# One list schedule over the whole kernel, changes of TensorE's tiling in its model, and a bank of its own for the last product

## The chip, the cores and the metric

The kernel runs on one core of one Trainium2 chip. The metric is the device time of one execution in microseconds (us); before the change it is 645.9 us, the median of three runs between 644.11 and 646.52. The profile of one further execution has a span of 646.7 us from the first to the last instruction. Times inside the kernel below are from that profile, counted from the start of its span.

## The reference, cut to what matters

Two blocks follow each other, all in 32-bit floats. The first is a linear recurrence over time for 4 batches and 8 heads of width 48, 768 steps long:

```python
for t in range(S):                      # state: (B, H, 48, 48)
    cur = einsum('bhd,bhe->bhde', u * k[t], v[t])
    y[t] = einsum('bhd,bhde->bhe', r[t], state + cur)
    state = w * state + einsum('bhd,bhe->bhde', k[t], v[t])
```

The second takes the result as 3072 tokens of 384 features, normalises each token and applies a gated layer of width 1536:

```python
xn = x / sqrt(mean(x * x) + 1e-6) * rms_g
out = (silu(xn @ w_gate) * (xn @ w_val)) @ w_out
```

## The kernel before: the parts that the change touches

Time is cut into 12 chunks of 64 steps, so a chunk is 256 tokens. For each chunk, a chain of small operations called *mixing* does the recurrence; its three large pieces on TensorE are named A (scores inside the chunk), Y (outputs) and U (the new state), and S stands here for the small products of the normalisation. Then the tokens go through the first layer in blocks here called R, and through the second in blocks called F. Chunks 0 and 1 are done one by one. Chunks 2 to 11 are done in five pairs, each with a form of Strassen's algorithm: seven products f1 to f7 for each of six groups of features, and seven products P1 to P7 for the second layer, in place of eight each.

The pieces of TensorE's work have four shapes, which the profile shows as rows times columns: A is 48\*64, Y is 128\*64 and 128\*48, U is 128\*48, R is 64\*128, and F and S are 128\*128. An R block is one product of the first layer:

```python
def product(ps_, w, x, start):
    for cc in range(CC):                 # 3
        for z in range(2):               # two halves of the rows
            rows = slice(64 * z, 64 * z + 64)
            pe.matmul(ps_[:, z, 0:NT], w[rows, cc, :], x[rows, cc, :], ...)
```

The order of all instructions is fixed when the program is built. Every operation is put into a list with its engine, an estimate of its cost, what it reads and writes; a list scheduler then simulates the engines, and picks on each engine the ready operation with the earliest deadline. Deadlines come backwards from *goals* for the products of the two layers:

```python
late = [goals.get(i, 1e6 + i) for i in range(n)]
for i in reversed(range(n)):
    for j in then[i]:
        late[i] = min(late[i], late[j] - self.hop(i, j) - self.ops[i][1])
```

There are two such lists, one after the other. The first (chunks 0 to 3 of mixing, chunks 0 and 1 of the layers, and the rounding of the weights) is improved by a random search over the goals; the second (all the pairs) is scheduled once:

```python
p.give(p.search(cells, 25.0, {"PE": 1.5, ...}, 3000), warm)

p = Plan()
... # all pairs; mixing and loads of the next pair go between the layers
p.give(p.schedule(p.goals_of(line, 0.0, 1.19), free, 0.5))
```

TensorE writes its products into six PSUM banks, two each named a, b and c, and two more for mixing. One group of a pair uses them like this (with VectorE's and ScalarE's readers left out except one):

```python
mm(xs_a, a_keys, a, wa[i][:, o], xa[s], True, "f1")
mm(["t2"], ["b"], b, late["s2"][i][:, o], t_of(2), True, "f2")
add("DVE", 0.69, ["b", "m1"], ["g1"], lambda: dve.tensor_add(gv[:, :, 1], b[sl], m1), name="g1")
mm(["t1"], ["c"], c, late["s1"][i][:, o], t_of(1), True, "f3")
mm(xn_a + [f"s3.{i}"], ["b"], b, wa[i + 2][:, o], xa[s + 1], False, "f4")
mm(xs_b, a_keys, a, wb[i][:, o], xb[s], False, "f5")
mm(["t4"], ["b"], b, wb[i + 2][:, o], t_of(4), False, "f6")
mm(xn_b, ["c"], c, late["s4"][i][:, o], xb[s + 1], False, "f7")
```

Here `t1`, `t2`, `t4` and the new `xa[s + 1]` are sums of the tokens of the pair, which VectorE makes after mixing. In the second layer of a pair:

```python
bank = {"x": bank_of["a"][:, 0], "w": bank_of["a"][:, 1], "y": bank_of["b"][:, 0], "z": bank_of["c"][:, 0]}
mm("x", h_keys[0], h[0], part(0, 0), True, "P1")
mm("z", gs + out_keys("o1"), sum_1, w2(0), True, "P5")
mm("x", h_keys[2], h[2], part(2, 0), False, "P2")
mm("y", ts + out_keys("o2"), sum_2, w2(1), True, "P6")
plus(["o1"], ["b", "m1"], results[:, 1], flat["y"], m1, "u2")
mm("y", h_keys[1] + out_keys("o3"), h[1], part(0, 1), False, "P7")
plus(["o3"], ["b", "m1"], results[:, 3], flat["y"], m1, "u3")
mm("w", h_keys[3] + out_keys("o4"), h[3], w2(2), True, "P4")
plus(["o2"], ["a1", "o3"], results[:, 2], flat["w"], results[:, 3], "c21")
plus(["o3"], ["c"], results[:, 3], flat["z"], results[:, 3], "c22")
mm("z", h_keys[2], h[2], part(2, 1), False, "P3")          # adds to P5 in the same bank
plus(["o1"], ["c"], results[:, 1], flat["z"], results[:, 1], "c12")
result(1, s, 1)                                            # the store to memory
```

P3 adds to the bank that holds P5, so it may start only when VectorE's `c22` has read P5 from there; `c22` comes after `u3`, which needs P7.

Of the kernel before, what the change touches and what calls it, by code (L numbers as in the profile page):

```python
# [50 lines left out]
P = 128  # L51
# [12 lines left out]
L = 64  # L64
# [30 lines left out]
class Plan:  # L95
# [3 lines left out]
    HOP = 0.2  # L99

    def __init__(self):
        self.ops, self.last, self.readers = [], {}, {}

    def add(self, engine, cost, reads, writes, give, land=0.0, port=False, name=""):
# [7 lines left out]
        self.ops.append((engine, cost, deps, give, land, port, name))  # L112
# [11 lines left out]
    def schedule(self, goals, free, patience=0.3):  # L124


        n = len(self.ops)
        then = [[] for _ in range(n)]
        for i, op in enumerate(self.ops):
            for d in op[2]:  # L130
                then[d].append(i)
        late = [goals.get(i, 1e6 + i) for i in range(n)]
        for i in reversed(range(n)):
            for j in then[i]:
                late[i] = min(late[i], late[j] - self.hop(i, j) - self.ops[i][1])
        free, port = dict(free), {"DVE": 0.0, "POOL": 0.0}
        missing = [len(op[2]) for op in self.ops]
# [4 lines left out]
        for _ in range(n):  # L142
            when, e = min((max(free[e], min(at[i] for i in ready[e])), e) for e in free if ready[e])
            i = min((i for i in ready[e] if at[i] <= when), key=lambda i: late[i])
            sooner = [j for j in ready[e] if at[j] <= when + patience and late[j] < late[i] - 1]
            if sooner:
                i = min(sooner, key=lambda j: late[j])
            s = max(when, at[i])
            if self.ops[i][5]:
                s = max(s, port["POOL" if e == "DVE" else "DVE"])  # L150
# [5 lines left out]
            for j in then[i]:  # L156
                at[j] = max(at[j], end[i] + self.hop(i, j))
                missing[j] -= 1
                if not missing[j]:
                    ready[self.ops[j][0]].add(j)  # L160
        return start

    def replay(self, start, free):

        free, port, end = dict(free), {"DVE": 0.0, "POOL": 0.0}, [0.0] * len(self.ops)
        for i in sorted(range(len(self.ops)), key=lambda i: (start[i], i)):
            e, cost, deps, _, _, locks, _ = self.ops[i]
            s = max([free[e]] + [end[d] + self.hop(d, i) + (1.0 if self.ops[d][0] == "SP" else 0.05) for d in deps])
            if locks:
                s = max(s, port["POOL" if e == "DVE" else "DVE"])  # L170
            free[e] = end[i] = s + cost * (1.0 if e == "PE" else 1.05)
            if locks:
                port[e] = end[i]
        return end
# [9 lines left out]
    def search(self, cells, first, free, trials):  # L184

        goals, rng, best = self.goals_of(cells, first, 1.0), random.Random(3), None
        for trial in range(trials):
# [5 lines left out]
            elif trial:  # L193
                new[rng.randrange(len(self.ops))] = rng.uniform(0, max(goals.values()))
            start = self.schedule(new, free)
            end = self.replay(start, free)
            end = max(end[i] for i in cells) + 0.3 * sum(end[i] for i in cells) / len(cells)
            if best is None or end <= best[0]:
                best, goals = (end, start), new
        return best[1]  # L200
# [13 lines left out]
def fast(ctx, tc, chan, tok, vpad, wka, wkb, wot, cols, u_row, out, bad):  # L214
# [417 lines left out]
    bank_keys = {"a": ["a0", "a1"], "b": ["b"], "c": ["c"]}  # L632
# [56 lines left out]
    def mixing(s):  # L689
# [3 lines left out]
        if quick:  # L693
            add("ACT", 1.6, ["w", "CHk0", "CHk1"], ["ku"], lambda: u_k(s, ku), name=f"ku {s}")
            for half in range(2):
                add(
                    "PE", 1.05, ["ku", "CHr0", "CHr1"], [f"a{half}"],
                    lambda half=half: products(bank_of["a"][:, half], half, ku, CH[:, 0], CH[:, 0]), name=f"E {s}",
                )
# [23 lines left out]
        if quick:  # L723
            for half in range(2):
                add("PE", 1.05, score_keys[half], [two[half][1]], lambda half=half: scores(half), name=f"A {s}")
        else:
            add(
                "PE", 2.35, score_keys[0] + score_keys[1], [two[0][1], two[1][1]], lambda: [scores(0), scores(1)],
                name=f"A {s}",
# [25 lines left out]
        else:  # L755
            add(
                "PE", 3.25, ["VSv"] + output_keys[0] + output_keys[1], [pair[0][1], pair[1][1]],
# [45 lines left out]
        for z in range(2):  # L803
# [3 lines left out]
            "PE", 1.9, ["KH0", "KH1", "VSv", "VSs0", "VSs1"] + [f"khd{z}{i}" for z in range(2) for i in range(HP)],  # L807
# [13 lines left out]
        "DVE", 0.86, ["pw"], ["o0"], lambda: [  # L821
# [4 lines left out]
    add("PE", 0.9, ["o0"], [key], lambda bank=bank: token_powers(bank), name="wk")  # L826
# [27 lines left out]
    def gate_val(s, i, o):  # L854
# [6 lines left out]
            lambda: product(ps_, wa[i][:, o], xa[s], True), name=f"g {s} {i} {o}",  # L861
# [3 lines left out]
            lambda: product(ps_, wb[i][:, o], xb[s], False), name=f"g {s} {i} {o}",  # L865
        ))
        add("ACT", 0.38, keys, [f"h{n}"], lambda: act.activation(h, ps_[:, 0, 0:NT], AF.Silu), name=f"silu {s}")
        add("DVE", 0.42, keys, [f"h{n}"], lambda: dve.tensor_mul(h, ps_[:, 1, 0:NT], h), name=f"hm {s}")
        return h, f"h{n}"

    def add_cell(s, i, hs):

        po, keys = next_bank()
        sums = rows_out[:, s]
# [9 lines left out]
        if i == 0:  # L884
            add("ACT", 0.8, keys, [f"o{s}"], lambda: act.copy(sums, po[:, :, 0:DM]), name=f"o {s}")
        else:
            add("DVE", 0.96, keys, [f"o{s}"], lambda: dve.tensor_add(sums, po[:, :, 0:DM], sums), name=f"o {s}")
# [693 lines left out]
```

## Time and profile before

| what | value |
|---|---|
| time, median of 3 | 645.9 us |
| span of the profile | 646.7 us |
| TensorE busy (of it matmuls of ones that only keep it busy in the first 25 us: 84 records) | 625.2 us |
| VectorE, ScalarE, GpSimd busy | 436.5, 349.0, 42.1 us |
| granted TensorE clock, mean | 0.991 |
| memory read and written | 58.69 MB and 4.72 MB |

Every operation is recorded through one helper, so all rows carry its line, L92; rows are told apart by the tiles they write and read and by their shapes. `bank_a`, `bank_b` and `bank_c` are written by the layers, `at` by mixing. TensorE is busy nearly all the time, so three things decide: the gaps in which it does nothing, the clock that it is granted, and whether its busy time is all needed. An idle time of another engine matters only where TensorE waits at its end.

### The profile page before, as it was taken

What the parts mean: (1) busy time and instruction counts of PE and PEld (TensorE: products, weight loads), DVE (VectorE), ACT (ScalarE), POOL (GpSimd) and SP (SyncE); (2) the same over time, 40 slices, a digit from 0 to 9 for tenths busy, and PEclk for the clock granted to TensorE, in tenths of its full rate; (3) what the DMA queues carried; (4) which work ended last, traced back from release to release, by engine and by line L of the source; (5) the groups of instructions that cost most, each with busy time, mean ns of one, the idle gap of its engine ahead of it and who ended that gap; (6) DMA issues with size and microseconds to landing.
All of it is one profiled execution on the core that took longest, in us unless ns stands there. A gap on an engine that the chain in (4) does not pass through costs nothing.

```text
span 646.7 us, 16003 instructions
## 1 busy us (share of the span) xinstructions
PE 625.2 (97%) x6882; PEld 549.6 (85%) x6882; DVE 436.5 (67%) x613; ACT 349.0 (54%) x914; POOL 42.1 (7%) x39
## 2 busy tenths in 40 slices
PE   9989999999999999999999999999999999899994
PEld 8868687877888998888898888898888899788894
DVE  7898877747785968774866666766676754555531
ACT  5796575634622878722887832696931694321200
POOL 3154440100000000000000000000000000000000
PEclk9989999999999999999999999999999999999997
DMA  8886641413200354600353501154501142100001
GB/s 261 303 303 220 185 153 51 117 47 88 107 11 2 111 168 121 190 22 1 82 201 98 166 1 66 51 170 148 153 27 50 43 118 63 35 1 1 2 15 41
DMA packets 21233, 64.54 MB, mean 100 GB/s; under 512 B 2720, under 2 KB 8480, under 8 KB 19744
## 3 DMA queue, kind: packets, MB, share of 16 engines
q1 hardware_dynamic: 21152, 63.42, 31.5%
q8 instruction: 56, 0.92, 0.6%
q14 instruction: 25, 0.20, 0.1%
HBM read 58.69 MB, written 4.72 MB: 98 GB/s over the span
## 4 chain that ended last, share of the span: by engine, by line
PE 88%; DVE 5%; DMA 3%; ACT 2%; issue 1%; SPq 0%; DVEq 0%; ACTq 0%
PE bank_b L92 29%; PE bank_a L92 25%; PE bank_c L92 23%; PE at L92 11%; DMA chan<-in_chan_dram 1%; DMA TOK<-in_tok_dram 1%; DVE rows_out L92 1%; DVE gv L92 1%; DVE ME L92 1%; ACT MO L92 1%; ACT ME L92 1%; DVE t L92 1%; DMA sq<-in_wot_dram 0%; DVE TOK L92 0%; DVE MO L92 0%
## 5 line engine op out<-in xcount | busy, mean ns | idle before, releaser
L92 DVE TENSOR_TENSOR gv<-bank_b,m 128x512 f32<-128x512 f32 x90 | 62.2, 691 | 47.8 <-PE bank_b L92 44.9
L92 PE MATMUL bank_b<-xa,wa 64*128 64x256 f32 x444 | 55.1, 381 | 3.6 <-DVE gv L92 2.4
L92 DVE TENSOR_TENSOR gv<-bank_c,gv 128x512 f32<-128x512 f32 x60 | 41.4, 690 | 16.2 <-PE bank_c L92 15.3
L92 PEld LDWEIGHTS bank_b<-xa,wa 64*128 64x128 f32 x444 | 42.0, 187 | 10.4 <-DVE gv L92 3.6
L92 ACT ACTIVATE gv<-gv 128x512 f32<-128x512 f32 (+1 forms) x60 | 30.7, 523 | 37.2 <-DVE gv L92 37.1
L92 ACT COPY m<-bank_a 128x512 f32<-128x512 f32 (+1 forms) x35 | 19.9, 570 | 56.9 <-DVE gv L92 42.9
L92 PE MATMUL bank_a<-xa,wa 64*128 64x256 f32 x396 | 49.1, 380 | 1.4 <-DVE rows_out L92 1.4
L92 PE MATMUL bank_a<-wo,h 128*128 128x192 f32 (+1 forms) x264 | 49.8, 345 | 0.5 <-ACT m L92 0.5
L92 ACT ACTIVATE sq<-sq 128x384 f32<-128x384 f32 x72 | 40.5, 562 | 16.9 <-DMA sq<-in_wot_dram 10.9
L92 PE MATMUL bank_a<-xb,wb 64*128 64x256 f32 x396 | 48.9, 379 | 0.0
L92 PEld LDWEIGHTS bank_a<-wo,h 128*128 128x128 f32 x264 | 43.2, 190 | 5.4 <-issue 1.3
L92 ACT ACTIVATE ME<-dmask,du 64x64 f32<-64x64 f32 x176 | 46.0, 331 | 2.8 <-DVE du L92 2.0
L92 ACT ACTIVATE MO<-dmask,du 64x64 f32<-64x64 f32 x176 | 46.7, 336 | 0.8 <-DVE du L92 0.2
L92 PE MATMUL bank_b<-t,s 64*128 64x256 f32 x360 | 44.1, 377 | 1.6 <-DVE t L92 1.6
L92 PE MATMUL bank_b<-t,wb 64*128 64x256 f32 x360 | 44.4, 379 | 0.0
L92 PE MATMUL bank_c<-xb,s 64*128 64x256 f32 x360 | 44.3, 378 | 0.0
L92 PEld LDWEIGHTS bank_a<-xa,wa 64*128 64x128 f32 x396 | 37.2, 187 | 8.1 <-DVE rows_out L92 3.0
L92 PE MATMUL bank_c<-t,s 64*128 64x256 f32 x360 | 44.1, 377 | 0.0
L92 ACT ACTIVATE gv<-bank_a 128x256 f32<-128x256 f32 x30 | 11.5, 384 | 58.2 <-PE bank_a L92 58.1
L92 PEld LDWEIGHTS bank_a<-xb,wb 64*128 64x128 f32 x396 | 37.8, 187 | 5.9 <-issue 1.8
L92 PEld LDWEIGHTS bank_b<-t,s 64*128 64x128 f32 x360 | 34.7, 187 | 6.0 <-DVE t L92 2.0
L92 PEld LDWEIGHTS bank_c<-xb,s 64*128 64x128 f32 x360 | 34.5, 187 | 5.1 <-issue 1.3
(143 smaller groups left out, 1289.3 us busy)
## 6 DMA issues: line engine op xcount, KB each, us to landing
chan<-in_chan_dram SPq DMA_DIRECT2D x11, 1024.0 KB, 6.8
TOK<-in_tok_dram SPq DMA_DIRECT2D x12, 768.0 KB, 4.8
VS<-in_vpad_dram SPq DMA_DIRECT2D x24, 336.0 KB, 4.9
raw<-in_wot_dram SPq DMA_DIRECT2D x8, 576.0 KB, 5.7
out_dram<-rows_out SPq DMA_DIRECT2D x48, 96.0 KB, 2.4
sq<-in_wka_dram SPq DMA_DIRECT2D x12, 384.0 KB, 3.0
sq<-in_wkb_dram SPq DMA_DIRECT2D x12, 384.0 KB, 3.2
sq<-in_wot_dram SPq DMA_DIRECT2D x12, 384.0 KB, 3.2
```

Of the source, the lines that this page charges most:

```text
L92: return lambda *args, **kwargs: self.tc.keep_in_program_order(give(*args, **kwargs))
```

## The change

1. **One schedule.** Both lists become one. The random search now looks at all operations up to the first product of the second pair, and is scored by the ends of all TensorE's operations; then everything is scheduled once. To make this possible many operations look up their tiles only when they are given out (`lambda: wa[i][:, o]`), and the keys of the tiles have the same names in both parts.
2. **Changes of tiling in the model.** Each TensorE operation is marked as using half the rows at a time (`rows=True`: R and A) or all of them (Y, U, F, S). A change of the mark costs 0.15 us in the model, and an operation that needs a change has to be more urgent by 2 us to be taken. The estimates for A, Y and U are lowered to 2.0, 2.85 and 1.58 us.
3. **Twice the time for the pairs' chains.** For operations of the pairs, deadlines are counted back with twice the cost and twice the hop between engines, so that long chains of small operations become urgent sooner.
4. **A bank for the last product.** P3 writes the second bank of c and no longer adds to P5 there; VectorE adds P5 in one operation more (`u4`). In the last pair P3 is given in two halves, each with its own addition and store, so that the first half's store can run beside the second half.

The purpose is that TensorE finds less time without work where one part meets the next, and changes its tiling less often.

The core of the diff (cuts are marked with `...`; left out are the renamed keys, the lambdas of point 1, and the moved lines around them):

```diff
     HOP = 0.2
+    SWITCH = 0.15
+    AHEAD = 30.0
+    KEEP = 2.0
...
-        for i in reversed(range(n)):
-            for j in then[i]:
-                late[i] = min(late[i], late[j] - self.hop(i, j) - self.ops[i][1])
+        early = min(goals[i] for i in goals if i >= relaxed) - self.AHEAD
+        for i in reversed(range(len(self.ops))):
+            by, cost = 2 if i >= relaxed else 1, self.ops[i][1]
+            for j, hop in self.then[i]:
+                due = late[j] - by * (hop + cost)
+                if i < relaxed <= j and due < early:
+                    due = early
+                if due < late[i]:
+                    late[i] = due
...
-            i = min((i for i in ready[e] if at[i] <= when), key=lambda i: late[i])
+            turn = (lambda i: late[i] + self.KEEP * (self.ops[i][7] != mode)) if e == "PE" else late.__getitem__
+            i = min((i for i in ready[e] if at[i] <= when), key=turn)
...
             s = max(when, at[i])
+            if e == "PE":
+                s += self.SWITCH * (self.ops[i][7] != mode)
+                mode = self.ops[i][7]
...
-        goals, rng, best = self.goals_of(cells, first, 1.0), random.Random(3), None
+        rng, best, last = random.Random(2), None, [i for i in range(count) if self.ops[i][0] == "PE"]
...
-                "PE", 2.35, score_keys[0] + score_keys[1], ..., name=f"A {s}",
+                "PE", 2.0, score_keys[0] + score_keys[1], ..., name=f"A {s}", rows=True,
...
-                "PE", 3.25, ["VSv"] + output_keys[0] + output_keys[1], ...     # Y
+                "PE", 2.85, ["VSv"] + output_keys[0] + output_keys[1], ...
...
-            "PE", 1.9, ["KH0", "KH1", "VSv", "VSs0", "VSs1"] + ...             # U
+            "PE", 1.58, ["KH0", "KH1", "VSv", "VSs0", "VSs1"] + ...
...
-    p.give(p.search(cells, 25.0, {"PE": 1.5, ...}, 3000), warm)
-    p = Plan()
...
-        keys = {"x": "a0", "w": "a1", "y": "b", "z": "c"}
+        keys = {"x": "a0", "w": "a1", "y": "b0", "z": "c0", "v": "c1"}
...
+        plus(["r1"], ["c0"], results[:, 1], flat["z"], results[:, 1], "u4")
...
-        mm("z", h_keys[2], h[2], part(2, 1), False, "P3")
-        plus(["o1"], ["c"], results[:, 1], flat["z"], results[:, 1], "c12")
-        result(1, s, 1)
+        for js in ((0, 1),) if s + 2 < NS else ((0,), (1,)):
+            mm("v", h_keys[2], lambda: h[2], part(2, 1), js[0] == 0, "P3", js)
+            to, x = (t[:, js[0] : js[-1] + 1] for t in (results[:, 1], flat["v"]))
+            plus(["r1"], ["c1"], to, x, to, "c12")
+            result(1, s, 1, js)
...
-    free = {"PE": 0.0, "DVE": 0.0, "ACT": 0.0, "POOL": 0.0, "SP": 0.0}
-    p.give(p.schedule(p.goals_of(line, 0.0, 1.19), free, 0.5))
+    goals = p.goals_of(cells, 25.0, 1.0) | p.goals_of(line, 150.0, 1.0)
+    n_searched = next(i for i in line if p.ops[i][6] == f"f1 {FIRST + 2} 0")
+    goals = p.search(cells, goals, free, n_searched, n_first, 3000)
+    p.give(p.schedule(goals, free, len(p.ops), n_first), warm)
```

## The prediction

> **What bounds the kernel now.** I read the busy times first, then TensorE's idle time and granted clock by stage, then the chain that ended last in order of time, and at the end the compiled order of TensorE's instructions in both kernels. The busy line:
>
> ```profile
> PE 625.2 (97%) x6882; PEld 549.6 (85%) x6882; DVE 436.5 (67%) x613; ACT 349.0 (54%) x914; POOL 42.1 (7%) x39
> ```
>
> TensorE is the bound; VectorE has a third of the span to spare. The work itself is not changed (258 R blocks, as many F blocks and as many A, Y and U in both compiled orders), so the change can only take from three things: the 21 us in which TensorE is idle, time under a lowered clock, and time lost inside the 625 us. The table by stage gives the first two (columns: length of the stage, busy time of each engine, granted clock, DMA share, GB/s):
>
> ```profile
> core 0: us, PE busy (x) PEld busy (x) DVE busy (x) ACT busy (x) POOL busy (x), PEclk, DMA share, GB/s
> 25.00:45.00 20.00, 16.37 (x287) 13.89 (x282) 18.08 (x25) 19.47 (x58) 7.71 (x7) 0.99 0.84 280
> 45.00:50.40 5.40, 5.40 (x14) 2.68 (x13) 5.30 (x9) 2.48 (x6) 3.06 (x3) 0.72 0.78 265
> 50.40:206.00 155.60, 155.60 (x1653) 127.06 (x1652) 115.98 (x160) 81.17 (x211) 24.14 (x16) 1.00 0.32 99
> 206.00:540.00 334.00, 330.21 (x3864) 298.58 (x3862) 229.05 (x303) 210.93 (x567) 0.00 (x0) 1.00 0.32 98
> 540.00:604.00 64.00, 61.38 (x534) 53.94 (x530) 34.71 (x56) 18.53 (x37) 0.00 (x0) 1.00 0.07 17
> 604.00:634.10 30.10, 27.16 (x172) 25.64 (x170) 12.87 (x15) 1.90 (x4) 0.00 (x0) 1.00 0.04 9
> 634.10:640.00 5.90, 5.85 (x24) 5.55 (x24) 0.00 (x0) 0.00 (x0) 0.00 (x0) 0.71 0.30 69
> ```
>
> Length minus PE busy is the idle time: 3.6 us in the opening, none from 45 to 206, 3.8 + 2.6 = 6.4 in the pairs, 2.9 in the last layer. From 634 the clock is 0.71. The chain shows what that means (columns: start, us, what):
>
> ```profile
> 624.45 3.90 PE bank_a L92 x24
> 628.35 3.91 PE bank_b L92 x24
> ...
> 632.28 0.57 DVE rows_out L92
> ...
> 632.93 0.57 DVE rows_out L92
> ...
> 633.52 0.57 DVE rows_out L92
> ...
> 634.13 5.86 PE bank_c L92 x24
> ```
>
> P7 ends at 632.26; then three additions of VectorE (`u3`, `c21`, `c22`) stand alone before P3, which waits 1.9 us for its bank. Then P3 itself takes 5.86 us where its like take 3.90.
>
> The third loss is also in the chain, at the seam of a pair (U between F blocks):
>
> ```profile
> 215.13 4.10 PE bank_a L92 x24
> 219.23 1.57 PE at L92 x64
> 220.81 4.10 PE bank_c L92 x24
> 224.90 3.90 PE bank_a L92 x24
> 228.80 3.90 PE bank_b L92 x24
> ```
>
> An F block takes 3.90 after another F and 4.10 after U. Elsewhere R takes 1.50 after F or A and 1.29 after R. So each change of shape costs 0.20 us, also where the rows stay at 128 (U, then F) and only the columns differ.
>
> **What the Trainium skill says.** "TensorEngine Tiling (Array Packing)", Key Properties: changing the tiling mode, not just the tile, drains TensorE. The trace agrees and gives the price, 0.20 us. "TensorE: Matmul & The Clock Gate", What's actually happening: the clock falls to half after an idle window of about 3.4 us, and comes back after a busy one of the same length. Here P3 lost 5.86 - 3.90 = 1.96 us after 1.9 us of idling, so part of a window was enough. "PSUM — Partial Sum Buffer", Summary: rules for kernel authors, advises that a reader of PSUM beside running matmuls take another bank; the 1.9 us wait for `c22` is what sharing cost.
>
> **The change, part by part.**
>
> *A bank for P3 and the new end.* The compiled order ends R, P1, P5, P6, P2, P7, half of P3, P4, the other half. Before it was R, P1, R, R, the small flag product, P2, P5, P6, P4, P7, P3. Gone with it: 2.9 us of idling (0.5 at the flag product, 0.6 before P6, which waits for `sum_2`, 1.9 before P3), of which I leave 0.3: P6 now comes 8 us after the last f7, and the sums behind f7 need 0.69 + 0.42 + 0.42 + 1.76 + 1.76 = 5.1 us plus hops. The second half of P3 waits for the first half's addition, but P4 (3.9 us) lies between. So -2.6. With no idling before it P3 keeps its clock: -2.0. Three changes of shape become one: -0.4. The last addition is half as long (0.56 before) and the last store half as large: -0.3. Sum **-5.3**. The remaining 6 us after it (store, landing, end of program) stay.
>
> *Twice the time for the chains.* Most of the 6.4 us of idling in the pairs is one thing: the second chunk's normalisation comes too late. Before, S of that chunk stood directly before the next pair's f1. In the last such seam S is at 544 us, and f2 and f4 wait until 554.9 and 557.3 for the sums of tokens: 13 us of chain (root, inverse, product, two copies, three sums, and in between a check of weights waiting 3.2 us for its DMA). In the new order five F blocks, 5 x 3.9 = 19.5 us, lie between that S and f1. 13 us fit in. The 1.0 us at 246 hangs on a load of `chan` that took 6.9 us; its deadline is earlier too. What I fear in return: in the new order A stands at the seam, then P1, Y, P6. From the end of f7 to P6 that is 2.0 + 4.1 + 2.9 = 9.0 us, in which VectorE must do the last group (0.69 + 0.42 + 0.69), four masks (4 x 0.75 = 3.0) and two sums (3.5): 8.3 us. That is tight. Behind U the order is A, three R, Y: 4.1 us for four masks between the additions that free bank b. I leave 1.5 us of idling: **-4.9**.
>
> *Fewer changes of shape.* I counted places in the compiled order where the shape changes (F and S are one shape): 115 before, 102 after. In the opening, before the first U, they go from 7 to 11, but there TensorE does filler work, so that costs nothing. In the last layer 3 become 1 (counted above). Between lie 105 before and 90 after. In the repeating pair it is 18 to 15: P3 no longer stands behind f1 (two changes) and A sits at the seam (one). 15 x 0.20 = **-3.0**. The model thinks that A among R, and Y and U among F, are free; by the trace they are not, so its 68 changes of rows after 80 before say less than my count.
>
> *The opening (2 to 50 us).* It loses 3.6 us of idling and about 1.5 us of clock (5.4 x 0.28). The search has another start and another score. In the new order TOK of chunk 0 is loaded before the weights and the masks come before the first rounding on VectorE, so the second load of TOK, which took 6.4 us and set the chain to Y of chunk 1, can start about 2 us earlier. But only two R blocks, not five, stand before that Y, so TensorE runs dry for about 4 us there, which may lower the clock for longer. I take **-0.5**, give or take 2.
>
> *The single schedule itself* gains nothing directly: from 45 to 206 us, where the two lists met, TensorE has no idle time.
>
> Sum: -5.3 - 4.9 - 3.0 - 0.5 = -13.7; the work added, one 0.55 us addition per pair on VectorE, is off the path. 645.9 - 13.7 = 632.2, and I say **632 us**.
>
> **The rivals.**
>
> *VectorE takes over at the seams.* For it: the 8.3 of 9.0 us above, four times, and bank b's additions during masks. Against it: 67% busy, and in the R stages before only 2.4 us were lost to those additions. It would give back 3 to 4 us: 636.
>
> *The opening gets worse.* For it: TensorE dry for 4 us before Y, and half clock after shorter idling twice in this trace. Against it: the chain there starts earlier. Worth up to +3: 635.
>
> *Waits were the only cost.* If a change of tiling only hides a wait, the 15 fewer changes give nothing: 635. Against it, the 0.20 us repeats to the hundredth.
>
> *All goes right*, the opening too, and no idling is left in the pairs: 629.
>
> **Range and chances.** A gain of 2% needs 633.0 or less, 12.9 of my 13.7 us. The end (5.3) and the changes (3.0) are sure to within 1 us; the pairs can miss by 2, the opening by 2, more easily on the slow side. I put 8 in 10 on 628.5 to 636. Faster by over 2%: 0.60; within 2%: 0.39; slower by over 2%: 0.01.
>
> **What the profile will show.** Right: the last eight blocks without a gap, the last P3 half in about 1.95 us and no lowered clock at the end; PE idle from 206 to the last layer 2 us or less; R and F blocks still 0.20 us longer after a change, and PE busy lower by about 5 us. Wrong: waits of TensorE for masks (`ME`, `MO`) or for `t` at the seams, a clock under 0.9 between 30 and 50 us, or a time at 50 us behind the old one for the same blocks done. The prediction fails most easily if the opening loses what the pairs gain, or if new waits of half a microsecond are strewn over the R stages.

## The result, and the profile after

The changed kernel takes 640.9 us (median of 4 runs, 639.88 to 641.75) against 646.2 us for the kernel before beside it (644.11 to 646.97): a ratio of 0.992 with an interval of 0.990 to 0.995. It is faster, by 5.3 us, not by the 13.7 us predicted, and lies outside the range. The profiled execution has a span of 638.1 us; it was the fastest of the four, and the one of before (648.5 us) stood 2.3 us above its median, so the two spans differ by more (8.6 us) than the medians do.

The busy line of the page and the table by stage of the kernel after (columns as in the prediction):

```profile
PE 619.1 (97%) x6880; PEld 550.2 (86%) x6880; DVE 437.3 (69%) x619; ACT 348.3 (55%) x914; POOL 41.2 (6%) x39
```

```profile
25.00:47.90 22.90, 17.70 (x306) 15.69 (x301) 20.86 (x28) 21.82 (x63) 9.58 (x8) 0.93 0.88 288
...
206.00:540.00 334.00, 333.45 (x3796) 304.51 (x3793) 232.50 (x316) 194.44 (x516) 0.00 (x0) 1.00 0.30 89
540.00:600.70 60.70, 60.70 (x543) 54.60 (x541) 28.90 (x48) 12.78 (x24) 0.00 (x0) 1.00 0.05 11
600.70:628.30 27.60, 27.60 (x172) 27.30 (x170) 11.23 (x13) 1.56 (x4) 0.00 (x0) 1.00 0.05 12
628.30:638.10 9.80, 0.04 (x2) 0.00 (x0) 0.83 (x3) 0.00 (x0) 0.00 (x0) 0.67 0.26 59
```

In the pairs TensorE now idles 0.6 us (it was 6.4), in the last layer not at all, and there the clock stays at 1.00. Two stages are worse. After TensorE's last instruction come 9.8 us in which it does nothing; before, from 639.98 to 646.73, it was 6.75:

```profile
640.00:646.70 6.70, 0.00 (x0) 0.00 (x0) 0.56 (x1) 0.00 (x0) 0.00 (x0) 0.65 0.16 37
```

And the opening loses 5.2 us of idling between 25 and 48 us, where before it was 3.6 us. What TensorE waits for there (columns: us in total, times, longest):

```profile
PE at L92 <- DVE MO L92: 3.7, 1, 3.7
PE bank_b L92 <- POOL wa L92: 1.5, 1, 1.5
```

`MO` is a mask product of the mixing of chunk 1, ahead of its Y: a wait that I had named as a sign of being wrong. `wa` are rounded weights.

A third view puts all of it on one scale. From the start times of the blocks in the trace I took, for each stretch, the time above what the blocks take undisturbed (R 1.295, F 3.90, and A, Y and U the same way), with 0.20 us for each change of shape. "Doubling alone" is a run of the experiments, the kernel before with point 3 of the change and nothing else:

| us lost | before | after | doubling alone |
|---|---|---|---|
| to 45 us | 8.0 | 10.8 | 6.9 |
| 45 to 206 us | 1.6 | 1.7 | 0.1 |
| pairs, 206 to 602 us | 8.0 | 1.4 | 1.4 |
| last layer, up to the last product | 3.3 | 0.1 | 1.2 |
| last product at half clock | 1.7 | 0 | 0 |
| changes of shape x 0.20 | 23.0 (115) | 20.4 (102) | 21.8 (109) |
| after TensorE's last instruction | 6.75 | 9.8 | 6.6 |
| span of the profile | 646.7 | 638.1 | 632.5 |

The differences of the columns add up to the differences of the spans within 0.6 us. Each column is one execution; that of the doubling alone was, like that of the change, the fastest of its four. The first two columns say where the change's gain came from (pairs, last layer, clock, changes of shape) and what it gave back (opening and end, 6 us). The third says that one line of the diff would have done more than all of it.

### The profile page after: what moved, and what is told of

Its sections match the earlier page's. It is cut to its first block, busy times and chain, and to the rows that moved or that the text cites. A ratio compares the mean times of both kernels' runs of the same rounds, so it can differ in the third digit from the quotient of the medians.

```text
span 638.1 us, 15980 instructions
## 1 busy us (share of the span) xinstructions
PE 619.1 (97%) x6880; PEld 550.2 (86%) x6880; DVE 437.3 (69%) x619; ACT 348.3 (55%) x914; POOL 41.2 (6%) x39
## 4 chain that ended last, share of the span: by engine, by line
PE 87%; DMA 4%; DVE 3%; ACT 3%; issue 1%; POOL 0%; SPq 0%; DVEq 0%; POOLq 0%; ACTq 0%
PE bank_b L92 28%; PE bank_a L92 26%; PE bank_c L92 23%; PE at L92 11%; DMA chan<-in_chan_dram 3%; DVE bits L92 1%; ACT MO L92 1%; DVE rows_out L92 1%; DMA sq<-in_wot_dram 1%; DMA sq<-in_wka_dram 0%; ACT ME L92 0%; ACT sq L92 0%; DVE ME L92 0%; DVE chan L92 0%; ACT VS L92 0%
## 5 line engine op out<-in xcount | busy, mean ns | idle before, releaser
L92 ACT ACTIVATE gv<-gv 128x256 f32<-128x256 f32 (+1 forms) x60 | 30.6, 521 | 37.0 <-DVE gv L92 36.6
L92 PEld LDWEIGHTS at<-ME,VS 128*64 128x64 f32 (+1 forms) x576 | 35.3, 135 | 7.3 <-DVE MO L92 4.1
L92 PE MATMUL at<-ME,VS 128*64 128x64 f32 (+1 forms) x576 | 37.3, 226 | 3.7 <-DVE MO L92 3.7
```

The source lines that it names most:

```text
L92: return lambda *args, **kwargs: self.tc.keep_in_program_order(give(*args, **kwargs))
```

## The experiments

All times are medians in us, and each ratio is to runs of the kernel before beside them on the same chip (medians 647.65 for e1 to e4, 646.91 for e5 to e8, 646.88 for e9 to e12, 644.21 for e13 to e16, 646.91 for e17 and e18). "Shapes" is the number of changes of shape.

| run | base and edit | time (lowest to highest, runs) | ratio, interval | shapes |
|---|---|---|---|---|
| e1 | after, P3 whole in the last pair | 639.55 (638.3 to 641.9, 6) | 0.989 (0.986 to 0.992) | 102 |
| e2 | e1, flag's product and load early | 639.71 (638.8 to 640.9, 6) | 0.988 (0.985 to 0.991) | 104 |
| e3 | after, old opening | 641.0 (638.9 to 642.3, 6) | 0.990 (0.987 to 0.993) | 103 |
| e4 | before, P3 in c's second bank | 649.38 (646.6 to 652.3, 22) | 1.004 (1.002 to 1.006) | 107 |
| e5 | after again | 641.41 (639.6 to 643.7, 12) | 0.992 (0.989 to 0.994) | 102 |
| e6 | after without the doubling | 655.76 (654.6 to 658.0, 6) | 1.015 (1.011 to 1.020) | 109 |
| e7 | e1, P3 back in P5's bank, opening's goals kept | 638.95 (638.0 to 639.6, 6) | 0.989 (0.985 to 0.993) | 111 |
| e8 | after, filler up to 40 us | 641.82 (640.0 to 644.1, 15) | 0.993 (0.990 to 0.995) | 105 |
| e9 | before, doubling alone | 636.02 (634.2 to 637.4, 4) | 0.985 (0.980 to 0.989) | 109 |
| e10 | e2, opening's goals kept | 639.59 (639.1 to 640.3, 6) | 0.989 (0.986 to 0.993) | 104 |
| e11 | e10, P3 of the last pair in b's second bank | 638.55 (637.1 to 639.4, 6) | 0.987 (0.984 to 0.991) | 104 |
| e12 | after, no tiling in the model | 646.55 (644.4 to 648.8, 14) | 0.999 (0.996 to 1.002) | 106 |
| e13 | e9 again | 635.82 (633.8 to 638.1, 4) | 0.987 (0.981 to 0.992) | 109 |
| e14 | e9, tiling in the model | 634.46 (632.4 to 637.3, 6) | 0.983 (0.979 to 0.988) | 109 |
| e15 | e9, P3 in b's second bank, early flag | 635.72 (633.3 to 637.9, 6) | 0.985 (0.981 to 0.989) | 111 |
| e16 | e11, old opening | 637.96 (635.7 to 640.4, 6) | 0.988 (0.984 to 0.992) | 105 |
| e17 | after, P3 in b's second bank in all pairs | 638.62 (638.3 to 639.6, 6) | 0.988 (0.986 to 0.991) | 102 |
| e18 | e16, P3 in b's second bank in all pairs | 635.73 (633.6 to 636.7, 6) | 0.983 (0.980 to 0.985) | 105 |

### What the doubling is worth: e6, e9, e13

e6 takes it out of the changed kernel's final schedule, e9 and e13 put it alone into the second list of the kernel before:

```diff
-            by, cost = 2 if i >= relaxed else 1, self.ops[i][1]      # e6, in after
+            by, cost = self.BY if i >= relaxed else 1, self.ops[i][1]
...
+    p.BY = 1
     p.give(p.schedule(goals, free, len(p.ops), n_first), warm)
```
```diff
-                late[i] = min(late[i], late[j] - self.hop(i, j) - self.ops[i][1])       # e9, in before
+                late[i] = min(late[i], late[j] - self.BY * (self.hop(i, j) + self.ops[i][1]))
...
     p = Plan()
+    p.BY = 2
```

> The changed kernel with deadlines of the pairs counted back with single cost and hop in the last scheduling (the search as changed, so the opening is the same). Theory 'chains late': S of the second chunk moves back to one P3 before the next pair's f1, and TensorE waits at the four seams again: 8 to 13 us of idling between 206 and 604 us instead of 1.4; the compiled order has 109 changes of shape after 102 (1.4 us), and the flag leaves the end (-1 us): 648 to 652. Rival 'the bank alone removed the waits': 641 to 642.

> The kernel before with one edit: in its second list (all the pairs) deadlines are counted back with twice the cost and twice the hop. Two lists, shared bank, no changes of tiling in the model, old opening, old end. Theory (the doubling is nearly the whole change): TensorE's waits between 206 us and the last layer fall from about 8 to about 2 us, the changes of shape from 115 to 109 (6 x 0.20 = 1.2 us), the end stays as before: about 640.5 against about 647, at or below the changed kernel. Rival (the doubling only works together with the single schedule and the tiling in its model): 645 to 647, waits in the pairs of 6 us or more.

> The kernel before with the doubling in its second list alone, once more, as the measure for the three runs beside it: 636, within 1.5 us. If the 636.0 was luck of the clock, 638 or more.

The changed kernel ran once more beside e6, as its measure:

> The changed kernel itself once more, beside the other three of this call, with a second profile. The before kernel's executions spread from 642.8 to 652.0 us and follow their granted clock (0.999 down to 0.985), so the single profile of before (648.5 us with its execution) and of the changed kernel (639.9) each show one draw. Theory 'clock by chance': the new profile differs from the first by stretches of 3.4 us at half clock in the opening and by little else; median 640.9 as before, single executions 639 to 642. Rival 'the profile pair is typical': the ratio to before is 0.987, as the two spans have it.

It takes 641.4 us. Without the doubling it takes 655.8 us, more than the kernel before. The waits of e6:

```profile
PE bank_b L92 <- DVE gv L92: 3.8, 7, 0.8
...
PE bank_b L92 <- DVE t L92: 2.7, 4, 1.2
```

These are the sums of tokens (`t`) and the groups' additions (`gv`) that come too late at every seam; the pairs lose 16.7 us in place of 1.4. Alone in the old structure the doubling takes 636.0 and, a second time, 635.8 us: 10.9 and 8.4 us less than before. It needs neither the one schedule nor the tiling in the model nor a bank. From e9's table by stage:

```profile
206.00:540.00 334.00, 333.73 (x3820) 302.59 (x3817) 233.27 (x313) 202.91 (x549) 0.00 (x0) 1.00 0.33 97
540.00:592.00 52.00, 52.00 (x472) 46.81 (x473) 25.46 (x42) 11.47 (x22) 0.00 (x0) 1.00 0.04 8
592.00:625.90 33.90, 32.72 (x216) 31.35 (x212) 13.39 (x16) 2.39 (x5) 0.00 (x0) 1.00 0.07 17
625.90:632.50 6.60, 0.03 (x1) 0.00 (x0) 0.56 (x1) 0.00 (x0) 0.00 (x0) 0.72 0.23 52
```

Idle in the pairs: 0.3 us. In the last layer 1.2 us are left, before P3, in place of 2.9. That shorter wait came with no half clock in this trace, P3 taking 4.17 us, and the way out after it is the old 6.6 us. So the other three parts of the change together cost about 5 us by the medians, 3 to 5 by the ratios. The rest of the study is the search for these.

### The end: e1, e2, e7, e10, e11, e15

```diff
-        for js in ((0, 1),) if s + 2 < NS else ((0,), (1,)):      # e1: P3 whole
+        for js in ((0, 1),):
```
```diff
-    flag()                                                        # e2: e1, and the flag early
+    loaded = flag()
...
+    goals[loaded] = goals[... f"f1 {NS - 2} 1" ...]
```
```diff
-            mm("v", h_keys[2], lambda: h[2], part(2, 1), js[0] == 0, "P3", js)   # e7: also P5's bank, no u4
+            mm("z", h_keys[2], lambda: h[2], part(2, 1), False, "P3", js)
```

> The changed kernel with P3 of the last pair in one piece, all else the same; the compiled order then ends P4, P3, flag product. Theory 'end': in the changed kernel 5.4 us pass between the last product and the last instruction of the store queue, because the stores of P4's sums and of P3's half queue up behind each other (six issues of about 0.6 us) and the flag is loaded after them; before it was 2.1 us. With P4 ahead of P3 only one addition (0.56), two issues (1.4) and the load of the flag (1.2) stay: 3.2 us, so 2 us less than the changed kernel, about 639. Rival 'the last landing decides': the span ends a fixed time after the last store lands, which one piece of double size makes later: same time or 0.3 us more. Rival 'noise': no difference that can be told, 641.

> As e1, and the flag product with its load stands in the first layer of the last pair instead of at the very end. Theory 'end': the load of the flag (1.2 us in the store queue) leaves the end, so 2.1 us stay there as before the change; on TensorE two changes of shape (0.4) and a wait of up to 0.6 us for the flag's load come in. Against e1: 1.2 less and 0.4 to 1.0 more, about 638.5 to 639; in the profile the time from the last product to the last instruction of the store queue is 2.1 us. Rival 'the last landing decides': the end is not shorter than in e1, and the time is 0.5 us above it.

> The changed kernel with P3 adding to P5 in its bank again (no u4, P3 whole), the same goals for the opening. Theory: the compiled order puts one R between P7 and P3 at each seam again (111 changes of shape, 9 more, 1.8 us); at the end P3 waits for u3, c21 and c22 (1.9 us) and in some executions loses 2 us of clock, while the flag product now stands before it; the doubled deadlines keep the rest of the seams free of waits: 640.9 + 3.7 to 5.7 = 645 to 646. Rival 'bank and doubling only work together', as the bank alone gained nothing in the kernel before: the idling between 206 and 604 us comes back too, 650. Rival 'the bank does nothing': 641.

The halves bring nothing: e1 is 1.4 to 1.9 us below the changed kernel's two medians (640.9, 641.4), but the intervals overlap. In its trace the way out is 8.7 us in place of 9.8. Moving the flag (the program's check of the weights: a small product, a copy to `bad`, and its load into registers) adds nothing to the time; the way out is 8.5 us. e7 gives up the own bank as well, with the flag's product ahead of P3, and is not slower, in spite of nine more changes of shape: its pairs lose nothing, where those of e1 lose 2.0 us. And the way out is the shortest of the three: 6.6 us from P3's end at 630.09 to the end of the span at 636.7. So what I called the gain of a bank doesn't show in the time. Why the way out is longer with it, VectorE's timeline of the changed kernel shows (start, us, operation, and in brackets the idle time before it and what ended it):

```profile
626.36 0.56 DVE L92 TENSOR_TENSOR rows_out<-bank_a,rows_out 128x384 f32<-128x384 f32 x1 [3.60 <-PE bank_a L92]
628.25 0.82 DVE L92 TENSOR_TENSOR rows_out<-bank_c,rows_out 128x384 f32<-128x384 f32 x2 [1.34 <-PE bank_c L92]
628.99 0.13 DVE L92 CAST bad<-at 1x1 int32<-1x1 f32 x1
```

The first row is `c21`. Behind it stands `c22`, which reads only P5's bank, and P5 is long finished. It starts at 628.25 all the same, when the last half of P3 ends, and `c12` runs straight after it: four stores are then still to be issued. The compiled program says why: `c22` waits there for TensorE, at a point after P3. P5's bank and P3's bank are two halves of one tile, `bank_c`, and the waits are kept by tile. e10 and e11 test this. e11 differs from e10 by one thing: in the last pair P3 writes the second bank of b.

```diff
-        keys = {"x": "a0", "w": "a1", "y": "b0", "z": "c0", "v": "c1"}
+        keys = {"x": "a0", "w": "a1", "y": "b0", "z": "c0", "v": "c1" if s + 2 < NS else "b1"}
```

> The changed kernel with P3 whole in the last pair, the flag's product and load moved into the last pair's first layer, and the goals of the opening kept as found (no new search). 104 changes of shape. In the compiled program VectorE's addition c22, which reads P5's bank, now waits for the end of P3, because both banks are one tile. Theory (the end after the last product is now the loss): no wait before P3, but two additions and four stores after it, 3.9 us from the end of TensorE to SyncE's branch: 638.5 to 639.5. Rival (changes of shape decide: 104 against the 111 of the shared bank's run, 7 x 0.2 = 1.4 us less): 637.5 or below in spite of that end.

> The run before it with one edit: in the last pair P3 writes the second bank of b, whose tile no waiting addition reads, in place of the second bank of c. In the compiled program c22 then waits for VectorE alone. Theory (a tile of two banks ties c22 to P3): c22 and its stores run beside P3, the way from the end of TensorE to SyncE's branch falls from 3.9 to about 2.0 us, the time by 1.9 us to about 637. Rival (the stores' queue or the landing sets the end anyway): the same time as the run before it, within 0.5 us.

The last rows of VectorE's timeline, first of e10, then of e11:

```profile
626.19 0.56 DVE L92 TENSOR_TENSOR rows_out<-bank_a,rows_out 128x384 f32<-128x384 f32 x1 [3.40 <-PE bank_a L92]
630.04 1.02 DVE L92 TENSOR_TENSOR rows_out<-bank_c,rows_out 128x384 f32<-128x384 f32 x2 [3.29 <-PE bank_c L92]
```

```profile
627.10 0.56 DVE L92 TENSOR_TENSOR rows_out<-bank_a,rows_out 128x384 f32<-128x384 f32 x1 [3.40 <-PE bank_a L92]
627.70 0.56 DVE L92 TENSOR_TENSOR rows_out<-bank_c,rows_out 128x384 f32<-128x384 f32 x1
630.95 0.56 DVE L92 TENSOR_TENSOR rows_out<-bank_b,rows_out 128x384 f32<-128x384 f32 x1 [2.69 <-PE bank_b L92]
```

In e11 `c22` runs at once, beside P3. The way out falls from 8.6 us (630.0 to 638.6) to 6.6 us (630.9 to 637.5), the 2 us expected; of the time 1.0 us came through, half of it, and the runs of the two overlap.

e15 puts this mended end (P3 in b's second bank, `u4`, the early flag) under the doubling alone:

```diff
-            mm("z", h_keys[2], h[2], part(2, 1), False, "P3")
+            mm("v", h_keys[2], h[2], part(2, 1), True, "P3")      # last pair, "v": the second bank of b
```

> The doubling alone plus a mended end: in the last pair P3 writes the second bank of b, and the flag's product and load stand in the first layer (111 changes of shape, two more). Theory: the 1.2 us wait before P3 goes, two changes of shape come (+0.4), the way out after P3 stays at 2.0 us: 635.2. Rival (half clock or the stores set the end): no gain, 636 or more.

Its P3 waits for nothing, but the time is e13's (635.7, 635.8): the rival holds. The 1.2 us before P3 were worth no measured time, with two changes of shape added and one profile at half clock in the opening.

### The opening: e3, e8, e16

e3 and e16 give the operations of the opening the start times that the kernel before has, in place of the search, and leave out the preference for a kept shape among them:

```diff
+OPENING = [ ... 437 start times ... ]
...
+        for i, t in enumerate(OPENING):
+            late[i] = t - 200.0
...
-    goals = p.search(cells, goals, free, n_searched, n_first, 3000)
```

e8 lets the matmuls of ones, which only keep TensorE busy, go on for longer:

```diff
-        if until < 27:
+        if until < 40:
```

> The changed kernel with the first list's operations in the order that they had before the change (their old start times as deadlines, no search); pairs and end as changed. Theory 'opening': the new search left TensorE dry before Y of chunk 1 (3.7 us of idling and 3.4 us at half clock), and cost 1.6 us up to the first second-layer block and 3 us up to 206 us; with the old order this comes back: 638 to 639.5. Rival 'the opening is bound by the loads and its order is chance': within 0.5 us of the changed kernel, 641.

> The changed kernel with the filler products (128x128, 0.11 us per pass) in modelled gaps up to 40 us instead of 27, which puts some 25 of them before A and Y of chunk 1. Theory 'opening clock': in the profile of the changed kernel TensorE is idle for 3.7 us before that Y, the clock halves from 37.7 to 41.1 us and Y takes 4.6 instead of 2.9 us; with filler the clock stays at full and 1.7 us come back per stretch avoided: 638 to 639.5, mean clock 0.003 to 0.006 higher. Rival 'it is the masks': Y ends when it did because filler delays it by two changes of shape and its own length: 641 to 642.

> The changed kernel with the old opening (fixed start times, no search) and the mended end (P3 whole, into the second bank of b, early flag); 105 changes of shape. Theory 1 (the opening and the end are the whole 5 us): as the doubling alone or better, 634.5 to 636. Theory 2 (in one schedule the time that an early chain saves is lost again at the seam to the first pair, as in the run with the old opening): 638 to 639, with waits of 3 us or more between 206 and 300 us.

e8 keeps TensorE busy and the clock at 1.00 from 25 to 52 us, and takes no less time (641.8 us), as its rival said. The mask that Y waits for is there at 38.1 us (36.6 in the trace of the change, 38.2 in e5), and behind the filler Y starts 0.9 us after it; without filler it starts at once. e3 is harder to read. The opening's loss falls by 3.3 us, to 7.5, but the time doesn't move, because 5.2 us are lost in the pairs where the changed kernel lost 1.4. e16, with the mended end, has the same: 638.0 us, as its second theory said. Of the 5.4 us that it loses in the pairs, 2.9 are idle time at the first seam, between 250 and 270 us. Two waits of TensorE make up most of them:

```profile
255.55 1.57 PE L92 MATMUL bank_c<-t,s 64*128 64x256 f32 x12 [0.52 <-DVE rows_out L92]
258.57 1.57 PE L92 MATMUL bank_b<-xa,wa 64*128 64x256 f32 x12 [1.46 <-DVE gv L92]
```

VectorE's timeline of e16 there:

```profile
246.41 0.95 DVE L92 TENSOR_TENSOR xa<-xb,xa 128x768 f32<-128x768 f32 x1
252.28 1.02 DVE L92 TENSOR_TENSOR rows_out<-bank_c,rows_out 128x384 f32<-128x384 f32 x2 [4.92 <-PE bank_c L92]
253.22 0.95 DVE L92 TENSOR_TENSOR t<-xb,t 128x768 f32<-128x768 f32 x1
254.08 0.95 DVE L92 TENSOR_REDUCE du<-TOK 128x16 f32<-128x768 f32 x1
254.94 0.55 DVE L92 TENSOR_TENSOR rows_out<-bank_c,rows_out 128x384 f32<-128x384 f32 x1
```

VectorE does nothing for 4.9 us. Next in its order are two additions that read `bank_c` (`u4` and `c22`), held until P3 ends. Behind them stand a sum of tokens (`t`), a step of the next mixing (`du`), and `c12`, which frees bank c. `c12` is the first of the two waits. The second is for the addition `gv`; that waits 2.3 us for ScalarE's copy `m`, which stands behind ScalarE's masks, and these need `du`. It is the tie of the end again. It is in every pair of the changed kernel too, and held VectorE for 4.05 us at this seam; but there `t` had been done just before, `du` was not behind it, and TensorE waited 0.5 us up to 268 us.

### The tie taken out of every pair: e17, e18

```diff
-        keys = {"x": "a0", "w": "a1", "y": "b0", "z": "c0", "v": "c1"}
+        keys = {"x": "a0", "w": "a1", "y": "b0", "z": "c0", "v": "b1"}
```

> The changed kernel with one edit: P3 writes the second bank of b in place of the second bank of c, in every pair (goals of the opening kept as found). In the compiled program u4 and c22 then no longer wait for the end of P3. The order of TensorE stays, 102 changes of shape. Theory (the tie costs where VectorE stands still): at the end c22 and its stores run beside the last half of P3 (about 1 us, the flag's product and load stay last), and 1 us of the waits of the pairs goes: about 639.3. Rival (VectorE has time to spare there): 640.5 or more.

> The run with the old opening and the mended end with one edit: P3 in the second bank of b in every pair, not in the last alone. Theory (the tie of c22 to P3 holds VectorE for 4.9 us at the first seam, and the token sum behind it is what TensorE waits for): the idle stretch of VectorE at 247 us goes, TensorE's waits between 206 and 300 us fall from 4.4 us to about 1, the time from 638.0 to about 634.5, as the doubling alone or better. Rival (the sums of the tokens come late for another reason): waits stay above 3 us, 637.5 or more.

e18's timeline at the same place:

```profile
246.68 0.95 DVE L92 TENSOR_TENSOR t<-xb,t 128x768 f32<-128x768 f32 x1
248.37 0.56 DVE L92 TENSOR_TENSOR rows_out<-bank_a,rows_out 128x384 f32<-128x384 f32 x1 [0.74 <-PE bank_a L92]
248.96 0.56 DVE L92 TENSOR_TENSOR rows_out<-bank_c,rows_out 128x384 f32<-128x384 f32 x1
...
250.56 0.95 DVE L92 TENSOR_REDUCE du<-TOK 128x16 f32<-128x768 f32 x1
252.27 0.56 DVE L92 TENSOR_TENSOR rows_out<-bank_b,rows_out 128x384 f32<-128x384 f32 x1 [0.76 <-PE bank_b L92]
```

`c22` no longer waits for P3 (the row at 248.96), `du` starts 3.5 us earlier and `c12` 2.7. The edit has also moved `t` ahead of `c22`, but TensorE didn't wait for `t`, as my theory had it; `du` and `c12` stand behind `c22` in both orders. TensorE's idle time between 206 and 300 us goes from 3.5 us in e16 to 0.7 in e18:

```profile
206.00:300.00 94.00, 90.50 (x1019) 81.17 (x1016) 68.10 (x93) 52.50 (x137) 0.00 (x0) 1.00 0.33 101
```

```profile
206.00:300.00 94.00, 93.31 (x1106) 84.56 (x1103) 70.92 (x97) 56.09 (x149) 0.00 (x0) 1.00 0.35 106
```

In time that is 2.2 us (638.0 to 635.7; the runs overlap), and in the changed kernel itself, with nothing else edited, 2.3 to 2.8 us (640.9 and 641.4 to 638.6), more than I expected. But the trace of e17 explains only part of that: its pairs lose 0.9 us, 0.5 less than in the trace of the change, and the way out is no shorter. Below stand the stage of e17 after its last product, and the issues of the last ten stores in the changed kernel (first row) and in e17 (second):

```profile
626.70:636.70 10.00, 0.01 (x1) 0.00 (x0) 0.34 (x2) 0.00 (x0) 0.00 (x0) 0.66 0.27 57
```

```profile
617.06 15.29 SPq L92 DMA_DIRECT2D out_dram<-rows_out  x10
615.44 14.51 SPq L92 DMA_DIRECT2D out_dram<-rows_out  x10
```

There P3 still comes in halves with the flag behind it. `c22` runs beside the last half, and the last store is issued 3.4 us after that half in place of 4.2 (629.95 and 632.35), yet the program ends 10.0 us after it; what holds the end the traces don't show. The 2 us of the tie came out at the end only where P3 was whole and the flag early (e10 to e11).

e17 and e18, run on the same chip in turn, differ by the opening and by the mended end, which shortens the way out from 10.0 to 7.5 us: together 2.9 us, with intervals that don't meet. (In e15 the mended end brought nothing, but there the way out was the old 6.6 us already.) No run takes the new opening out alone with the tie gone. The traces can say what it costs. Counted as in the table, nine profiles with the new search (all but e8 and e12) lose up to 206 us on average 4.3 us more than the nine with the old opening, and 3.2 us more than the three of these in one schedule (e3, e16, e18). Single profiles scatter by several us around that with their half-clock windows; between those of e17 and e18 it is 1.0 us.

With the tie gone, the end mended and the old opening back, the one schedule stands where the doubling alone stands (635.7 and 635.8). So the missing 5 us lie in these three. Some 3 are the opening by the traces; how the end and the tie in the pairs share the rest is not shown.

### The tiling in the model: e12, e14

e12 takes both constants out of the changed kernel's final schedule; e14 adds them, with the marks of A and R, to the second list of e9.

```diff
+    p.SWITCH, p.KEEP = 0.0, 0.0                            # e12
     p.give(p.schedule(goals, free, len(p.ops), n_first), warm)
```
```diff
-    p.BY = 2                                               # e14
+    p.BY, p.SWITCH, p.KEEP = 2, 0.15, 2.0
```

> The changed kernel with both constants of the tiling in the model at 0 in the final schedule (goals of the opening kept as found): 106 changes of shape in place of 102, the rest of the change whole. Theory (only the count matters): 4 x 0.20 = 0.8 us more than the changed kernel, about 641.9. Rival (the preference also keeps the chains apart, so waits return without it): 644 or more, with waits of TensorE over 5 us in the pairs. Second rival (the model costs waits of its own): 640 or below.

> The doubling alone plus the tiling in the model of the second list (0.15 us for a change, preference 2 us). The compiled order has 109 changes of shape, as without. Theory (the model gains only by the count of changes): the same as the doubling alone, within 1 us. Rival (the preference costs waits, and is part of the 5 us): 638 or more, with waits of TensorE above 3 us between 206 us and the last layer. Second rival (it avoids waits, as its removal from the changed kernel suggests): 634.5 or less.

e12 has only four more changes of shape, but takes 646.6 us. The chain of waits shows what was lost (start, us, what):

```profile
151.60 2.04 PE at L92 x64
153.63 0.02 issue
153.65 5.56 DMA chan<-in_chan_dram
159.21 0.02 issue
159.23 1.23 DVE chan L92
```

In this order the load of `chan` starts only when A is done, at 153.65, VectorE needs it before it has landed, and TensorE waits 2.9 us behind that. The loss from 45 to 206 us is 6.5 us in place of 1.7; the pairs are as good as with the model. So the rival's time came out, but not its place, and the theory by the count of changes (641.9) is wrong: taking the preference out moved other things, and a late load cost more than four changes. e14 gives the cleaner comparison. With 109 changes in both it is 1.4 us below e13, but the runs of the two overlap (632.4 to 637.3, 633.8 to 638.1), and whether the preference gains anything by itself stays open. e14 is the lowest median of all; by its ratio it is level with e18. Both beat the kernel before by 1.7%, and the changed kernel by 5 us or more.

### A bank alone: e4

e4 gives P3 a bank of its own in c, with `u4`, in all pairs of the kernel before, and nothing else.

```diff
+        plus(["o1"], ["c"], results[:, 1], flat["z"], results[:, 1], "u4")
...
-        mm("z", h_keys[2], h[2], part(2, 1), False, "P3")
+        mm("v", h_keys[2], h[2], part(2, 1), True, "P3")          # "v": the second bank of c
```

> The kernel before with nothing but P3's own bank (P3 whole, u4 added; old lists, old model, old search). Theory 'end': P3 no longer waits for three additions (1.9 us) and keeps its clock (2.0 us), and at the four seams P3 no longer stands behind f1, so 115 changes of shape become 107 (1.6 us): 646.2 - 5.5 = 640.7, as much as the whole change brought; what the doubled chains bring would then have been lost again in the opening and at the end. Rival 'the idling at the end was covered by stores': only the changes of shape, 644.5. Rival 'the changes of shape only hide waits': 642.3.

It is slower than before by 0.4%, and its loss in the pairs is 12.9 us against 8.0. That fits the tie, but e4 has no counterpart in bank b, so for the old order the cause is argued and not shown.

## Why the prediction was wrong, point by point

In the two profiles the gains came as forecast or larger: 6.6 us in the pairs (-4.9), 4.9 in the last layer and its last product (-2.6 and -2.0), 2.6 for changes of shape (-0.4 and -3.0). Two steps failed and gave back 5.9 us: the way out after the last product, which was to stay as it was, and the opening. The other 3.3 us between the spans' difference and the medians' are the draw of two single executions.

**The end (-5.3): half right, and one clause of it failed.** The idling before P3 and the half clock went as predicted; the last half of P3 takes 1.96 us and follows without a gap. "The remaining 6 us after it (store, landing, end of program) stay" failed: they became 9.8 us. I had read the compiled order of TensorE alone, and to its last product; what VectorE waits for behind it was in the same compiled program. And behind the last half the changed kernel still makes the flag's product, which I had cut off. Step by step the traces give 9.8 us as built, 8.7 with P3 whole (e1), 8.5 to 8.6 with the flag early too (e2, e10), and 6.6 with P3 in the other tile (e11). So the largest share, 2.0 us, is the bank that I credited with the gain: it lies in the tile of the bank that it was meant to be free of. The halves, from which I expected 0.3 us, cost about 1. One reading was wrong besides: P6 did not wait 0.6 us for `sum_2`, which was done at 616.3 us; the view puts that wait, up to 620.3, down to the flag's `bad`, done at 619.7. The wait went all the same, with the flag.

**Twice the time for the chains (-4.9): right in kind, sized too small.** Alone it is worth 8.4 to 10.9 us in the old structure, about double what I counted, and the changed kernel without it is 14.3 us slower. In the pairs themselves the trace loses 6.6 us less, where I counted 4.9. I counted only the idle time that the table shows (6.4 us); the blocks hid 1.6 us more. And part of what I gave to the bank was the doubling's: with it, P7 and P4 change places ahead of P3, P3 waits 1.2 us and not 1.9, and kept its clock in the trace.

**Fewer changes of shape (-3.0): the price holds, the gain by itself isn't shown.** The 0.20 us repeats in every trace, and 13 fewer changes are 2.6 us of the table. But no run moved by its count of changes: e7 has 111 and is no slower than e1 with 102, and e12's four more, 0.8 us by that price, are not what makes it 5 us slower.

**The opening (-0.5): wrong sign.** It costs 2.8 us in the table up to 45 us, and 3 to 4 in the averages over the traces. I had seen the pieces: that "only two R blocks, not five, stand before that Y, so TensorE runs dry for about 4 us" (it waits 3.7). Against it I set a chain starting about 2 us earlier, and that term failed: Y of chunk 1 starts at 36.66 us and started at 37.33, 0.7 us earlier, with about 3.9 us of R blocks still to be done afterwards.

**The single schedule gains nothing directly: right as far as the runs go.** e18 has it, with the tiling in the model and the bank, e13 has none of them, and they agree to 0.1 us (by their ratios e18 is 0.4% lower, with overlapping intervals).

**The rivals.** "The opening gets worse" happened, at about the size that I gave it (+3). "VectorE takes over at the seams" happened at one seam in another form: VectorE is not busy there, it is held, idle for 4 to 5 us before one addition. I had compared its work with the time, and not asked what its order makes it wait for.

**The starting point.** One profile is one execution. The 2.0 us at half clock that I counted as sure stand in a profile 2.3 us above the median. Whether the median execution has such a window at P3 the runs don't show, since only the profiled ones have a trace; the prediction was for the median.

## What to carry to other kernels

When a change has four parts, try each alone: here one line was worth more than the whole. A bank of its own is only free if the waits are kept by bank: look in the compiled program for what the reader waits for, above all on VectorE, where in these traces one held addition held everything behind it. Follow the end of the program on every engine up to the last store, and do not stop at the last product.

## What the runs showed of the hardware

The time of an execution goes with the granted clock. Over the 94 executions of the kernel before that ran beside the experiments, with mean clocks from 0.983 to 0.999, time and clock correlate with -0.84, and 0.01 of clock goes with 6.3 us. While TensorE works, the half clock comes in windows of 3.41 us or two or three of them together (6.83 in e16, 10.24 in e10), and where they fall changes with the execution: in one trace of the changed kernel a window starts at 37.7 us, in another (e5) two start at 24.5 and 38.1. "TensorE: Matmul & The Clock Gate" of the Trainium skill, What's actually happening, says that the window is free-running and advises against fitting a kernel to one count of slow instructions; these runs agree. A wait of 1.9 us before P3 was followed by such a window in the profile of before, and one of 1.2 us by none in the two profiles of the doubling alone.
